# An adaLN transformer block in float32: the normalization's inverse root by GpSimd's power, and five product banks of the gated unit as one ring

## The chip, the core and the metric

The kernel runs on one core of a Trainium2 chip. A core has a matrix engine (TensorE, PE in the profile; its weight loads are listed apart as PEld), a vector engine (VectorE, DVE), a scalar engine for table functions (ScalarE, ACT), a general engine (GpSimd, POOL) and a queue engine (SyncE, SP). Each engine takes its instructions in order from its own queue, and they wait for one another by semaphores. [...] The metric is the time of one execution on the device in microseconds, as the median of several runs.

## What is computed

A block of a transformer with 2048 tokens of width 576: a conditioned layer normalization, full attention with 32 heads of width 18, a residual, a second conditioned normalization, a gated linear unit with 4608 hidden columns, and a second residual. All arrays are float32. Cut to what matters:

```python
def _layernorm(x, axis=-1, eps=1e-5):
    m = jnp.mean(x, axis=axis, keepdims=True)
    v = jnp.var(x, axis=axis, keepdims=True)
    return (x - m) / jnp.sqrt(v + eps)

mod = (_silu(c) @ w_mod).reshape(c.shape[0], 6, 1, -1)
sa, ca, ga, sb, cb, gb = (mod[:, i] for i in range(6))
h = _layernorm(x) * (1 + ca) + sa
qkv = h @ wqkv                                  # 32 heads of 18
p = softmax(q @ k.T * 18 ** -0.5)
x = x + ga * ((p @ v) @ wo)
h = _layernorm(x) * (1 + cb) + sb
x = x + gb * ((sigmoid(h @ w_gate) * (h @ w_up)) @ w_down)
```

## The kernel before

**Number format.** PE multiplies in a reduced float32 format, so most operands are split into a high part and a low part (the rest), and a product is made of three partial products.

**Start (the first 230 us).** Tokens lie in 16 tiles of 128 rows, four tiles to a chunk. `normalized(ch)` (L344) loads a chunk, takes mean and variance of each row on VectorE (`ln_stats`), the inverse root for the four tiles at once (`ln_scales`, L159, which runs `ln_scales_steps`, L163, to its end), and scales the rows (`ln_apply`, L179: VectorE at L181, and a small copy on GpSimd at L184). `ln_transpose` (L186) turns the chunk on PE (L192), and ScalarE and VectorE make from it the columns of `hT`. Then follow the projections to queries and keys (L274) and values (L325). PE's order in this stage is planned by the scheduler when the kernel is compiled: a list scheduler that takes instructions by priority, in the order of the program, as they come ready by its own estimates.

**Attention (about 230 to 1600 us).** 32 units of 16 steps. PE's order is written out by hand here (`manual_schedule` on PE, L888), by strings of letters in the loop at L906: `t` a score product (L927) with its exponential on ScalarE (L931), `m` a score product for the row maxima of a later unit (L446) with its reduction on VectorE (L452), `v` a group of eight value products (L548), and `w`, once in two steps, a turn of background work. All score products take their banks from a turn of seven. The background work is a set of generators; `first_rows` (L755) projects the attention's outputs of the first eight tiles, takes their statistics, calls `ln_scales_steps` for eight tiles at once (L762) and then normalizes and transposes the rows. Each `yield` in it hands the turn back.

**Gated unit (about 1600 us to the end).** The hidden columns are done in 18 blocks of 256, for each half of the tokens. A block's four quarter products are formed by seven products instead of eight, by sums and differences of operands, in the order `ORDER = (1, 6, 2, 7, 5, 4, 3)`; each is a gate product and an up product of seven matmuls (L1028), into two banks. `banks` (L1188) takes the pairs: `a` at product 1, accumulated again at 2 and read by the gate (L1037, L1038); `b_` at product 6, accumulated at 7 and 4 and read after each (L1212, L1223, L1234); `c` at product 5, accumulated at 3 and read after each (L1228, L1239). `a` and `c` come from a tag `x` with three banks, `b_` from two tags, `bg` and `bu`, with one bank each. The other three banks, tag `d`, take the down products (L1064), which VectorE adds to the result (L1068). Weights for a product are prepared three products ahead by GpSimd, ScalarE and VectorE (L1008, L1019, L1020, L1021) and in the first half stored for the second. PE's order is the scheduler's for the first 56 products (`ORDERED = 56`) and the program's from there on. In between, every second product, runs a generator `last_rows` (L1108): the output projection of the last columns, two calls of `ln_scales` (L1168) with four tiles each, and the operands of the second half.

**What the change touches.** `ln_scales_steps`, which is called seven times (four chunks at the start, once in attention, twice in `last_rows`); the two constants at L69; the loop at L762 that steps it in attention; and `banks` with its three callers. In `ln_scales_steps` the variance plus 1e-5 goes to `var` (VectorE), ScalarE takes its square root, and VectorE the reciprocal `r0` and one Newton step for the inverse root, `rs = r0 (1.5 - 0.5 var r0^2)`.

Of the kernel before, what the change touches and what calls it, by code (L numbers as in the profile page):

```python
# [15 lines left out]
F32 = mybir.dt.float32  # L16
F32R = mybir.dt.float32r
AF = mybir.ActivationFunctionType
ALU = mybir.AluOpType
# [4 lines left out]
P = 128  # L24
# [10 lines left out]
EPS = 1e-5  # L35
# [20 lines left out]
def tile_block(ctx, tc, x_in, wqkv, wo, w_gate, w_up, w_down, c_in, w_mod, out):  # L56
    nc = tc.nc
# [3 lines left out]
    const = ctx.enter_context(tc.tile_pool(name="const", bufs=1))  # L61
# [4 lines left out]

    ident = const.tile([P, P], F32, name="ident")
    make_identity(nc, ident)
    eps = const.tile([P, 1], F32, name="eps")  # L69
    nc.vector.memset(eps, EPS)  # L70
    mcol = const.tile([P, 2, 5], F32, name="mcol")
    mcol2 = const.tile([P, 2, 6], F32, name="mcol2")
    gb_b = const.tile([P, D], F32, name="gb_b")
# [9 lines left out]
    def bank():  # L83

        turns["bank"] += 1
        return ps.tile([P, 512], F32, name=f"s{turns['bank'] % 7}")
# [66 lines left out]
    def ln_stats(pool, xt, mv):  # L153
        st = pool.tile([P, 2, nc.vector.BN_STATS_DIM], F32, name="st", bufs=2)
        for g in range(2):
            nc.vector.bn_stats(st[:, g, :], xt[:, g, :] if len(xt.shape) == 3 else xt[:, g * HALF : (g + 1) * HALF])
        nc.vector.bn_aggr(mv, st)
# [5 lines left out]
    def ln_scales_steps(pool, mv, rs):  # L163

        n = rs.shape[-1]
        var = pool.tile([P, n], F32, name="var")
        nc.vector.tensor_scalar_add(var, mv[:, :, 1], EPS)
        sd = pool.tile([P, n], F32, name="sd")
        nc.scalar.activation(sd, var, AF.Sqrt)
        yield  # L170
        r0 = pool.tile([P, n], F32, name="r0")
        nc.vector.reciprocal(r0, sd)

        nc.vector.tensor_mul(sd, r0, r0)
        nc.vector.tensor_mul(sd, sd, var)
        nc.vector.tensor_scalar(sd, sd, -0.5, 1.5, op0=ALU.mult, op1=ALU.add)
        nc.vector.tensor_mul(rs, r0, sd)

    def ln_apply(z, xt, mean, rs):  # L179

# [206 lines left out]
    def temp(shape, dtype):  # L387
        temps["n"] += 1
        return qpool.tile(shape, dtype, name=f"t{temps['n'] % 2}")
# [113 lines left out]
    with tc.tile_pool(name="wv1", bufs=1) as wvp:  # L503
        tiles = [[(o + D * w, P)] for o in (128, 256, 384) for w in (0, 1)] + [[(DM, 64), (D + DM, 64)]]
        for i, parts in enumerate(tiles):
# [5 lines left out]
            for g in range(2):  # L511
                pl = project_qk([(wt, 2 * g), (wt, 2 * g + 1)], run if i else None)
                col, n = parts[-1]
# [20 lines left out]
    bgp = bgs.enter_context(tc.tile_pool(name="bgp", bufs=1))  # L534
# [65 lines left out]
    mv2 = const.tile([P, NT, 2], F32, name="mv2")  # L600
    rs2 = const.tile([P, NT], F32, name="rs2")
# [153 lines left out]
    def first_rows():  # L755
        yield from load_wo()
        for t in range(8):
            yield from project_o(t)
        for t in range(8):
            ln_stats(bgp, Oa[:, t, :], mv2[:, t, :])  # L760
            yield
        for _ in ln_scales_steps(bgp, mv2[:, 0:8, :], rs2[:, 0:8]):  # L762
            yield
            yield
        yield

        def normalized_part(i, g, r):

            z = bgp.tile([P, 4, P], F32, name="z", bufs=2)
            c0 = g * HALF + i * P  # L770
            for j in range(4):
                t = 4 * r + j
                if i < 2:
                    to, x1 = z[:, j, :], Oa[:, t, c0 : c0 + P]
                else:
                    to = z[:, j, :].rearrange("p (n c) -> p n c", c=32)
                    x1 = Oa[:, t, c0 : c0 + 32].unsqueeze(1).to_broadcast([P, 4, 32])
                nc.gpsimd.tensor_scalar(
                    to, x1, mv2[:, t, 0:1], rs2[:, t : t + 1], op0=ALU.subtract, op1=ALU.mult
                )  # L780
            return z

        held = {"n": 0}

        def parts():
            n = held["n"] = held["n"] + 1
            return held["parts"][n % 3] if n % 3 < 2 else bgp.tile([P, 2, 512], F32R, name="ho")

        order = [(i, g, r) for i in range(3) for g in range(2) for r in range(2)]
        z = normalized_part(*order[0])  # L790
        yield
        for n, (i, g, r) in enumerate(order):
            if not g and not r:
                four = temp([P, 4, 512], F32)
                ho = temp([P, 4, 512], F32R)
            pt = bank()
            for j in range(4):
                nc.tensor.transpose(pt[:, j * P : (j + 1) * P], z[:, j, :], ident)
            c = 3 * g + i
            nc.vector.tensor_scalar(  # L800
                four[:, 2 * g + r, :], pt, mcol2[:, 0, c : c + 1], mcol2[:, 1, c : c + 1],
                op0=ALU.mult, op1=ALU.add,
            )
            if n + 1 < len(order):
                z = normalized_part(*order[n + 1])
            yield
            if g and r:
                held["parts"] = ho[:, 0:2, :], ho[:, 2:4, :]
                blocks = [four[:, j, :] for j in range(4)] + [bgp.tile([P, 512], F32, name="t3")]
                yield from operand_parts(  # L810
                    0, i, blocks, parts, nc.gpsimd.tensor_copy, nc.gpsimd, nc.gpsimd
                )
# [79 lines left out]
    for u in range(UNITS):  # L892
# [6 lines left out]
        for kt in range(NT):  # L899
# [6 lines left out]
            for does in (("vtmmttmvtm", "tmttkwmtmm") if plain else ("vmmttmmtvt", "mtkttmwmmt"))[kt % 2]:  # L906
# [16 lines left out]
                else:  # L923
                    c, h = next(sides)
# [8 lines left out]
            if u in (1, 3):  # L933
                if kt == 2:
                    a = big.tile([P, 8, 640], F32, name="big")
                    a = a.rearrange("p a b -> p (a b)")[:, 0 : 8 * D].rearrange("p (t c) -> p t c", t=4)
# [109 lines left out]
    def down_weights(st):  # L1046
        wd = wdp.tile([P, 2, 2, D], F32R, name="wd")
        nc.sync.dma_start(wd.rearrange("p l t d -> p (l t d)").bitcast(F32), wds[st["b"]].bitcast(F32))
        st["wd"] = wd[:, 0], wd[:, 1]
# [44 lines left out]
    def prepare(n):  # L1094
        if n < len(seq):
            weights_operand(block(n), seq[n][2])
            at = n % 7
            if at in (1, 3):
                load(n // 7 + 1, at // 2)
# [5 lines left out]
    pg = ctx.enter_context(tc.tile_pool(name="pg", bufs=1, space=PSUM))  # L1105
# [79 lines left out]
                    nc.sync.dma_start(t, hs[g, i, :, cols])  # L1185
                yield from operand_parts(1, i, blocks, parts, nc.scalar.copy, nc.vector, nc.sync)

    def banks(*names):  # L1188
        return [pg.tile([P, 512], F32, name=n, bufs=3 if n == "x" else 1) for n in names]

    def half(t, v):
        return t[:, 512 * v : 512 * (v + 1)]
# [3 lines left out]
    for n, (hf, b, k) in enumerate(seq):  # L1196
        if n == ORDERED:
            manual.enter_context(tc.manual_schedule(engines={mybir.EngineType.PE}))
        prepare(n + LOOK)
        st = block(n)  # L1200
        if k == 1:
            st["a"] = banks("x", "x")
            product(st, 1, st["a"], True)
            st["p1"] = ep.tile([P, 1024], F32, name="p1")
            for v in range(2):
                nc.scalar.copy(half(st["p1"], v), st["a"][v])
        elif k == 6:
            st["b_"] = banks("bg", "bu")
            product(st, 6, st["b_"], True)
            st["u2"] = ep.tile([P, 1024], F32, name="u2")  # L1210
            for v in range(2):
                nc.vector.tensor_add(half(st["u2"], v), st["b_"][v], half(st["p1"], v))  # L1212
        elif k == 2:
            product(st, 2, st["a"], False)
            for r in range(2):
                st["hh", r] = ep.tile([P, 2, 512], F32R, name=f"hh{r}")
                st["hl", r] = ep.tile([P, 2, 512], F32R, name=f"hl{r}")
            gate(st, None, 0, 0)
        elif k == 7:
            product(st, 7, st["b_"], False)  # L1220
            st["u3"] = ep.tile([P, 1024], F32, name="u3")
            for v in range(2):
                nc.vector.tensor_add(half(st["u3"], v), st["b_"][v], half(st["p1"], v))  # L1223
        elif k == 5:
            st["c"] = banks("x", "x")
            product(st, 5, st["c"], True)
            for v in range(2):
                nc.vector.tensor_add(half(st["u3"], v), st["c"][v], half(st["u3"], v))  # L1228
            gate(st, st["u3"], 1, 1)
            down_weights(st)  # L1230
        elif k == 4:
            product(st, 4, st["b_"], False)
            for v in range(2):
                nc.vector.tensor_add(half(st["p1"], v), st["b_"][v], half(st["p1"], v))  # L1234
            gate(st, st["p1"], 1, 0)
        else:
            product(st, 3, st["c"], False)
            for v in range(2):
                nc.vector.tensor_add(half(st["u2"], v), st["c"][v], half(st["u2"], v))  # L1239
            gate(st, st["u2"], 0, 1)  # L1240
        if n >= 5 and n % 2:
            next(rows2, None)
        if before is not None and k in (6, 7):
            down(before, k - 6)
        if k == 3:
            before = st
        if hf == 0 and b == NB - 1:
            s = ORDER.index(k)
            nc.gpsimd.dma_start(X[s], xs[1, s])
# [30 lines left out]
```

## Time and profile before

| what | value |
|---|---|
| median of 3 runs | 2932.16 us (2930.02 to 2932.91) |
| the profiled execution's own time | 2929.86 us |
| its span, first to last instruction | 2927.5 us |
| instructions | 46356 |
| mean granted clock of TensorE | 0.995 |
| bytes moved by DMA | 429.25 MB |

By stage, from the profile's stretches (us busy of each stretch):

| stretch, us | PE | VectorE | ScalarE | GpSimd |
|---|---|---|---|---|
| 0 to 30 | 15.4 | 17.8 | 9.3 | 10.7 |
| 30 to 100 | 67.1 | 45.2 | 25.5 | 19.6 |
| 100 to 270 | 164.7 | 107.3 | 53.5 | 39.5 |
| 270 to 1000 | 719.0 | 651.6 | 650.0 | 213.9 |
| 1000 to 1605 | 596.3 | 499.6 | 505.2 | 173.5 |
| 1605 to 1700 | 86.7 | 72.0 | 28.7 | 24.2 |
| 1700 to 1850 | 147.8 | 123.4 | 56.6 | 39.2 |
| 1850 to 2200 | 332.4 | 282.9 | 118.8 | 100.8 |
| 2200 to 2927.5 | 718.9 | 418.9 | 133.8 | 28.0 |

How to read the profile's lines. A group has the line of the program, the engine, the operation, out <- in with partitions x elements, the count, then busy time in us and the mean of one in ns, and last the idle time of the engine just before these instructions and what ended it. A row of the timeline begins with its start and its duration in us; the bracket at its end is the time that the engine stood idle before it and what released it. A row of waits has the total in us, how often, and the longest. A row of the stretches has the stretch and its length, then the busy time of PE, PEld, VectorE, ScalarE and GpSimd with the count of instructions, the granted clock of TensorE (1.00 is full speed), the busy share of the DMA engines and GB/s. The ends of matmuls are modelled, and a busy PE isn't PE at its peak.

### The profile page before, as it was taken

The numbers are of one execution on the slowest core, as the hardware profiler recorded it, in microseconds if no ns is written. First come the engines' busy times: TensorE is split into PE (matmuls) and PEld (weight loads), VectorE is DVE, ScalarE is ACT, GpSimd is POOL, SyncE is SP. The second block draws the span as 40 slices with busy tenths as digits, with TensorE's granted clock in tenths as the row PEclk, the third lists the DMA queues.
The fourth block names the chain that finished last, engine by engine and source line by source line (L and its number), as shares of the span: only waits on it lengthen the run. The fifth ranks groups of instructions, "written<-read, shape, count | busy, mean of one in ns | idle before, by whom it ended". The sixth has DMA issues, their size and how long they took to land.

```text
span 2927.5 us, 46356 instructions
## 1 busy us (share of the span) xinstructions
PE 2848.3 (97%) x17141; PEld 1879.6 (64%) x17141; DVE 2218.6 (76%) x4023; ACT 1581.4 (54%) x2955; POOL 649.4 (22%) x829
## 2 busy tenths in 40 slices
PE   7999999999999999999999899999999999999998
PEld 6964333333444444444443788877888888888888
DVE  7277888888899988999982878789777555555555
ACT  3216889999987778998788333333332111111111
POOL 3122014544213110761102222233221100000000
PEclk9999999999999999999999999999999999999999
DMA  5344124333212110222125866677556844554443
GB/s 180 120 157 128 52 76 140 133 120 123 84 56 76 35 56 23 101 98 66 52 87 177 284 216 234 231 277 247 207 201 233 301 170 167 167 168 167 159 159 136
DMA packets 136745, 429.25 MB, mean 147 GB/s; under 512 B 18884, under 2 KB 56520, under 8 KB 124232
## 3 DMA queue, kind: packets, MB, share of 16 engines
q1 hardware_dynamic: 120472, 344.99, 35.0%
q0 software_dynamic: 16048, 81.31, 7.9%
q8 instruction: 135, 2.21, 0.3%
q14 instruction: 90, 0.74, 0.1%
HBM read 267.77 MB, written 157.95 MB: 145 GB/s over the span
## 4 chain that ended last, share of the span: by engine, by line
PE 82%; DVE 7%; ACT 4%; DMA 3%; issue 3%; SPq 1%; POOL 0%; POOLq 0%; ACTq 0%; DVEq 0%
PE o L548 16%; PE d L1064 14%; PE x L1028 12%; PE s L446 11%; PE s L927 10%; PE bu L1028 4%; PE bg L1028 4%; PE s L274 4%; ACT p L931 3%; PE s L325 2%; PE s L685 2%; DVE mx L452 1%; DVE w L1020 1%; DMA B<-hs 1%; PE s L572 1%
## 5 line engine op out<-in xcount | busy, mean ns | idle before, releaser
L452 DVE TENSOR_REDUCE mx<-s 128x1 f32<-128x512 f32 x1696 | 1076.6, 684 | 126.3 <-PE s L446 108.3
L931 ACT ACTIVATE p<-s 128x512 f32<-128x512 f32 x2048 | 1068.4, 610 | 146.7 <-PE s L446 75.2
L446 PE MATMUL s<-k,q 54*128 54x512 f32 x1920 | 608.4, 451 | 12.2 <-ACT p L931 6.6
L548 PE MATMUL o<-p,vaug 128*32 128x512 f32 x4096 | 554.8, 607 | 0.5 <-ACT p L931 0.4
L927 PE MATMUL s<-q,k 56*128 56x512 f32 x1920 | 552.6, 425 | 1.3 <-DMA q<-mrows 0.8
L1064 PE MATMUL d<-wd,hh 128*128 128x288 f32 x2304 | 468.3, 297 | 20.8 <-DVE Oa L1068 20.2
L927 PEld LDWEIGHTS s<-q,k 56*128 56x128 f32 x1920 | 260.5, 186 | 295.2 <-DVE mx L452 184.7
L446 PEld LDWEIGHTS s<-k,q 54*128 54x128 f32 x1920 | 273.6, 184 | 250.3 <-ACT p L931 172.3
L1064 PEld LDWEIGHTS d<-wd,hh 128*128 128x128 f32 x2304 | 373.4, 188 | 35.6 <-DVE Oa L1068 26.4
L1068 DVE TENSOR_TENSOR Oa<-Oa,d 128x288 f32<-128x288 f32 x576 | 256.0, 452 | 125.5 <-PE d L1064 120.3
L1064 PE MATMUL d<-wd,hl 128*128 128x288 f32 x1152 | 340.7, 296 | 0.0
L1028 PE MATMUL x<-k,w 128*128 128x512 f32 x1008 | 242.4, 390 | 4.7 <-DVE u L1239 2.4
L1040 ACT ACTIVATE u<-u 128x512 f32<-128x512 f32 x72 | 45.5, 632 | 318.3 <-DVE u L1228 312.1
L1064 PEld LDWEIGHTS d<-wd,hl 128*128 128x128 f32 x1152 | 216.9, 188 | 0.0
L1028 PEld LDWEIGHTS x<-k,w 128*128 128x128 f32 x1008 | 186.7, 188 | 42.5 <-DVE u L1239 3.5
L548 PEld LDWEIGHTS o<-p,vaug 128*32 128x32 f32 x4096 | 83.4, 108 | 163.9 <-issue 151.4
L1037 ACT ACTIVATE sg<-x 128x512 f32<-128x512 f32 x36 | 21.5, 599 | 304.3 <-PE x L1028 304.3
L1070 POOL DMA_DIRECT2D out_dram<-Oa x16 | 8.7, 543 | 606.0 <-DVE Oa L1068 606.0
L455 ACT ACTIVATE over<-s 128x512 f32<-128x512 f32 x176 | 105.1, 597 | 33.5 <-PE s L446 28.4
L1028 PE MATMUL x<-big,w 128*128 128x512 f32 x504 | 120.6, 390 | 1.0 <-issue 1.0
L1028 PE MATMUL x<-w,w 128*128 128x512 f32 x504 | 121.0, 390 | 0.0
L457 DVE CUSTOM_DVE_ANT_0 over<-s,over 128x512 f32<-128x512 f32 x176 | 120.2, 683 | 0.3
(232 smaller groups left out, 3605.1 us busy)
## 6 DMA issues: line engine op xcount, KB each, us to landing
ws<-w SPq DMA_DIRECT2D x126, 640.0 KB
w<-ws SPq DMA_DIRECT2D x126, 640.0 KB
wd<-wds SPq DMA_DIRECT2D x36, 1152.0 KB
k<-kd SPq DMA_DIRECT2D x60, 360.0 KB
wds<-w POOLq DMA_DIRECT2D x18, 1152.0 KB, 4.5
k<-kd SPq DMA_DIRECT2D x60, 180.0 KB
w<-in_B_w_down_dram POOLq DMA_DIRECT2D x18, 576.0 KB, 4.3
q<-qd SPq DMA_DIRECT2D x64, 144.0 KB
```

The source lines that it names most:

```text
L274: nc.tensor.matmul(acc, w, hT[:, t, cols], start=n == 0, stop=n == len(ts_) - 1)
L325: nc.tensor.matmul(acc[:, 0:HALF], hT[:, k, rows], w, start=n == 0, stop=n == len(ts_) - 1,)
L446: nc.tensor.matmul(sp, qs[rows, qt * P : (qt + 1) * P], ks[rows, at * 512 : (at + 1) * 512], start=True, stop=True,)
L452: nc.vector.tensor_reduce(to, sp, axis=AX.X, op=ALU.max)
L455: nc.scalar.activation(over, sp, AF.Relu)
L457: nc.vector.tensor_tensor_reduce(out=over, in0=sp, in1=over, scale=1.0, scalar=LOWEST, op0=ALU.add, op1=ALU.max, accum_out=mx[:, h * n + q ...
L548: nc.tensor.matmul(acc[32 * j : 32 * j + 32, :], vaug[:, kt, (2 * p + h) * VW : (2 * p + h) * VW + 32], probs[2 * c + h], start=kt == 0, s ...
L927: nc.tensor.matmul(sT, ks[rows, kcols], qs[rows, c * 512 : (c + 1) * 512], start=True, stop=True)
L931: state["exp"] = nc.scalar.activation(pr, sT, AF.Exp, scale=SCALE)
L1028: nc.tensor.matmul(acc[v], w[:, v, a, :], X[s][:, b, :], start=first and n == 0, stop=n == 6, skip_group_check=not first,)
L1064: nc.tensor.matmul(acc[:, :HALF], a[:, f, rows], w[:, f, cols], start=n == 0, stop=n == 5)
L1068: nc.vector.tensor_add(Oa[:, t, cols], Oa[:, t, cols], acc[:, :HALF])
```

## The change

The Sqrt activation and the reciprocal are replaced by one GpSimd instruction that raises `var` to the power in a constant tile `powers` (-0.5, eight columns, filled once by GpSimd at the start; the unused `eps` tile goes). Its result `r0` is refined by two Newton steps on VectorE instead of one, eight instructions in place of four and the reciprocal. The generator now yields after the power and after each Newton step; in attention the loop that yielded twice for each of its steps becomes a plain `yield from`, so that the turns from the variance to the first normalized part are three, as before. The five banks of the products get one tag: pairs are taken from five banks in the order of the program.

```diff
-    eps = const.tile([P, 1], F32, name="eps")
-    nc.vector.memset(eps, EPS)
+    powers = const.tile([P, 8], F32, name="powers")
+    nc.gpsimd.memset(powers, -0.5)
...
         var = pool.tile([P, n], F32, name="var")
+        sd = pool.tile([P, n], F32, name="sd")
+        r0 = pool.tile([P, n], F32, name="r0")
         nc.vector.tensor_scalar_add(var, mv[:, :, 1], EPS)
-        sd = pool.tile([P, n], F32, name="sd")
-        nc.scalar.activation(sd, var, AF.Sqrt)
+        nc.gpsimd.tensor_tensor(r0, var, powers[:, 0:n], op=ALU.pow)
         yield
-        r0 = pool.tile([P, n], F32, name="r0")
-        nc.vector.reciprocal(r0, sd)
-
-        nc.vector.tensor_mul(sd, r0, r0)
-        nc.vector.tensor_mul(sd, sd, var)
-        nc.vector.tensor_scalar(sd, sd, -0.5, 1.5, op0=ALU.mult, op1=ALU.add)
-        nc.vector.tensor_mul(rs, r0, sd)
+        for to in (r0, rs):
+            nc.vector.tensor_mul(sd, r0, r0)
+            nc.vector.tensor_mul(sd, sd, var)
+            nc.vector.tensor_scalar(sd, sd, -0.5, 1.5, op0=ALU.mult, op1=ALU.add)
+            nc.vector.tensor_mul(to, r0, sd)
+            yield
...
-        for _ in ln_scales_steps(bgp, mv2[:, 0:8, :], rs2[:, 0:8]):
-            yield
-            yield
-        yield
+        yield from ln_scales_steps(bgp, mv2[:, 0:8, :], rs2[:, 0:8])
...
-    def banks(*names):
-        return [pg.tile([P, 512], F32, name=n, bufs=3 if n == "x" else 1) for n in names]
+    def banks():
+        return [pg.tile([P, 512], F32, name="x", bufs=5) for _ in range(2)]
...
-            st["a"] = banks("x", "x")
+            st["a"] = banks()
...
-            st["b_"] = banks("bg", "bu")
+            st["b_"] = banks()
...
-            st["c"] = banks("x", "x")
+            st["c"] = banks()
```

## The prediction

> **What bounds the kernel now.** I began with the busy times on the profile's page.
>
> ```profile
> PE 2848.3 (97%) x17141; PEld 1879.6 (64%) x17141; DVE 2218.6 (76%) x4023; ACT 1581.4 (54%) x2955; POOL 649.4 (22%) x829
> ```
>
> TensorE (PE) is busy for 97% of the span, and every other engine has room. Work taken from ScalarE (ACT) or added to VectorE (DVE) or GpSimd (POOL) therefore counts only where PE waits for it; only some 80 us of the span are PE idle. So I went to the places of the two edits. First the groups of ScalarE, where the square root shows by its table loads.
>
> ```profile
> L169 ACT ACT_TABLE_LOAD x4 | 5.1, 1283 | 0.1
> L931 ACT ACT_TABLE_LOAD x2 | 2.6, 1283 | 4.0 <-DMA kd<-kd_p 4.0
> L1037 ACT ACT_TABLE_LOAD x2 | 2.6, 1283 | 0.0
> ...
> L1040 ACT ACT_TABLE_LOAD x1 | 1.3, 1283 | 0.0
> ```
>
> L169 is the Sqrt. Its four loads go, and with them the loads that bring back Exp (one of L931's two) and Sigmoid (one of L1037's two and that of L1040): seven loads of 1.283 us, 9.0 us of ScalarE. Whether PE feels them is read from the timeline. Only one pair lies in the attention stage:
>
> ```profile
> 1107.95 1.28 ACT L169 ACT_TABLE_LOAD   x1
> 1109.24 0.21 ACT L169 ACTIVATE sd<-var 128x8 f32<-128x8 f32 x1
> 1109.47 1.28 ACT L931 ACT_TABLE_LOAD   x1
> 1110.76 0.60 ACT L931 ACTIVATE p<-s 128x512 f32<-128x512 f32 x1
> ```
>
> For 2.8 us no exponential runs. The timeline of PE over the same time shows what that does; x8 is one group of value products, two of which belong to each pair of steps.
>
> ```profile
> 1103.79 1.06 PE L548 MATMUL o<-p,vaug 128*32 128x512 f32 x8
> ...
> 1108.84 1.06 PE L548 MATMUL o<-p,vaug 128*32 128x512 f32 x8
> 1109.83 0.49 PE L927 MATMUL s<-q,k 56*128 56x512 f32 x1
> 1111.41 0.50 PE L446 MATMUL s<-k,q 54*128 54x512 f32 x1 [1.09 <-ACT p L931]
> ...
> 1117.37 1.07 PE L548 MATMUL o<-p,vaug 128*32 128x512 f32 x8
> ```
>
> A pair of steps takes 1108.84 - 1103.79 = 5.05 us; the pair with the table loads takes 1117.37 - 1108.84 = 8.53 us. So 3.5 us are lost there, though PE's one marked wait is 1.09 us. The rest shows in the stretches by window (the seventh number is the granted clock):
>
> ```profile
> 33.00:37.00 4.00, 3.91 (x16) 3.92 (x17) 4.00 (x19) 0.30 (x2) 0.01 (x1) 0.50 0.76 270
> 1113.00:1117.00 4.00, 4.00 (x17) 1.45 (x19) 2.36 (x6) 2.28 (x5) 4.00 (x6) 0.57 0.02 4
> 1605.00:1700.00 95.00, 86.68 (x474) 74.86 (x473) 71.97 (x123) 28.69 (x41) 24.23 (x23) 1.00 0.80 273
> ```
>
> After the stall the clock was 0.57 for four microseconds: a stall is followed by slow matmuls.
>
> **The change, part by part.** *Sqrt out, in the attention stage.* Both loads and the Sqrt leave ScalarE: -3.5 us by the two cadences (by ScalarE's own 2.8 us alone it would be -2.8). The other Sqrt loads lie at the start (ScalarE then waits for inputs) and in the gated stage, where ScalarE is idle most of the time, so I give them nothing; without that cover each would cost PE its 1.28 us.
>
> [...]
>
> *The power in.* The trace has no power on GpSimd. The nearest rows are an ordinary two-input instruction and GpSimd's longest single one:
>
> ```profile
> L591 POOL TENSOR_TENSOR Oa<-oT,rec 128x144 f32<-128x144 f32 x32 | 13.1, 433 | 171.2 <-ACT oT L587 170.9
> ...
> L364 POOL MEMSET vaug<- 128x9936 f32 x1 | 8.4, 8383 | 0.0
> ```
>
> A power of 4 or 8 elements per partition takes p, between under 0.43 and 8.4 us. In size it is nearest to the first row, but a power is many operations per element, so I take p = 1.0 us for every site and keep both ends. It is issued on POOL's in-order queue, which is mostly empty at each of the seven sites (22% busy). The new wait is on VectorE: the first Newton product waits for POOL where the reciprocal waited for ScalarE. Behind it on VectorE's queue stand, by stage, the normalization itself, the row maxima (which free PE's score banks) and the adds of the down products (which free PE's bank ring d). In attention the wait before was
>
> ```profile
> 1109.48 0.20 DVE L172 RECIPROCAL r<-sd 128x8 f32<-128x8 f32 x1 [0.29 <-ACT sd L169]
> ```
>
> so 0.7 us may be added at p = 1; the row maxima have some play, and I take +0.4 (0 to 0.7).
>
> *Newton's second step.* Eight VectorE instructions follow where there were five:
>
> ```profile
> L177 DVE TENSOR_TENSOR rs<-r,sd x7: 145/161/168, 10.7 to 1842.3; 128x4 f32<-128x4 f32 x6, 128x8 f32<-128x8 f32 x1
> ```
>
> Three more at 0.16 us are 0.5 us per site. The chain from variance to scale grows by p - 0.2 (the Sqrt) + 0.5 = 1.3 us. At the start this chain feeds PE's transposes of each chunk through the last POOL copy:
>
> ```profile
> 11.54 1.71 POOL L184 COPY x<-x 128x64 f32<-128x64 f32 x4 [1.96 <-DVE x L181]
> ...
> 36.99 1.71 POOL L184 COPY x<-x 128x64 f32<-128x64 f32 x4 [23.74 <-DVE x L181]
> 50.24 1.71 POOL L184 COPY x<-x 128x64 f32<-128x64 f32 x4 [11.54 <-DVE x L181]
> ...
> 65.48 1.70 POOL L184 COPY x<-x 128x64 f32<-128x64 f32 x4 [4.95 <-DVE x L181]
> ```
>
> ```profile
> 18.62 0.77 PE L192 MATMUL s<-ident,x 128*128 128x128 f32 x5
> ...
> 39.08 2.35 PE L192 MATMUL s<-ident,x 128*128 128x128 f32 x20
> ...
> 51.89 2.34 PE L192 MATMUL s<-ident,x 128*128 128x128 f32 x20
> ...
> 67.86 2.34 PE L192 MATMUL s<-ident,x 128*128 128x128 f32 x20
> ```
>
> The copies end at 13.25, 38.70, 51.95 and 67.18, so the transposes have 5.4, 0.4, 0 and 0.7 us to spare: 1.3 us more makes them late by 0, 0.9, 1.3 and 0.6, together 2.8. PE's order here is planned when the kernel is compiled, and value projections that need no new chunk can go ahead of the transposes, so I take half, +1.4 (0 to 2.8).
>
> [...]
>
> At the last rows, in the gated stage, two sites get 0.5 us more of VectorE each. VectorE already makes PE wait there:
>
> ```profile
> PE d L1064 <- DVE Oa L1068: 20.2, 22, 2.9
> ```
>
> I take +0.5 (0 to 2.6, if the 0.8 us of waiting for the power is paid too). In attention the three instructions are hidden: VectorE is 76% busy.
>
> *The ring.* Pairs of banks are taken in the order a, b_, c. Before, bank a[1] of a block reused the bank of c[0] of the block before, which is read only after product 3, the product just ahead; with five in turn b_[1] follows c[0], one product later, and no other bank gets a shorter lead than it had. The timeline has this wait once, at the first change of block:
>
> ```profile
> 1620.02 1.89 PE L1028 MATMUL bu<-big,w 128*128 128x512 f32 x7 [2.65 <-DVE u L1223]
> ...
> 1629.62 0.69 DVE L1239 TENSOR_TENSOR u<-x,u 128x512 f32<-128x512 f32 x1
> ...
> 1630.37 1.89 PE L1028 MATMUL x<-k,w 128*128 128x512 f32 x7 [2.38 <-DVE u L1239]
> ...
> 1635.51 0.63 PE L1124 MATMUL d<-ident,od 128*128 128x128 f32 x4 [1.66 <-DMA od<-oend]
> ```
>
> PE would save 2.4 us at 1630.37. But what is late next is the transpose at 1635.51, which waits for a load, seen in the chain of waits:
>
> ```profile
> 1628.49 6.89 DMA od<-oend
> ```
>
> It is issued by SP's queue at 1628.49 and lands at 1635.4 whatever the ring does; PE would wait there 4.0 us instead of 1.7. So I take 0. The other wait (2.65 us) is for reading a bank before its next accumulation, which a ring doesn't change. Yet PE's order of the first 56 products is planned at compile time, and another bank rule gives another order. The ends: both waits vanish (-5.0), or as much is added (+5.0); the stretch from 1605 to 1700 holds 95 - 86.7 = 8.3 us of PE idle in all.
>
> *Sum:* -3.5 + 0.4 + 1.4 + 0.5 + 0 = -1.2 us. The profiled execution took 2929.86 us (span 2927.5), which is 2.3 us under the median of 2932.16 and just under the lowest run shown, 2930.02. Against its own time the forecast is 2928.7; against the median, 2931.0, and that is my number.
>
> **Rivals.** *A, the ring pays (faster).* The new order of the first products removes both waits: -1.2 - 5.0, and the chunks at the start are filled wholly (-1.4): 2924.6 us. For it: the bank waits stand in the trace. Against: the load that is late next.
>
> *B, the power is slow (slower).* Every site has VectorE waiting in order behind POOL. By the terms above the time grows with p: attention p - 0.3, half of the three unspared chunks (3 (p + 0.3) - 1.1) / 2, half of two last sites p + 0.3, less 3.5: together 3.5 p - 3.6. It cancels the gain at p = 1.0, is slower by over 0.2% from p = 2.7, and at p = 4 gives +10.4, 2942.6 us; at 8.4 it gives 2958. For it: POOL has no such operation in the trace, and 1 us is only chosen. Against: few elements.
>
> *C, the start stalls and the clock falls.* PE's wait before 33.09 was followed by a clock of 0.50 from 33 to 37, 2 us of lost work:
>
> ```profile
> 33.09 0.85 PE L325 MATMUL s<-wv_h,hT 128*128 128x288 f32 x2 [2.62 <-DVE pl L281]
> ```
>
> If nothing fills the chunks (2.8 instead of 1.4) and two of the three late transposes are followed by such a stretch, that is 5.4 us more: 2936.4; with a worse order of the first products, up to 2941.4.
>
> *D, the loads stay*, because another function needs the table that the Sqrt brought in: +3.5, 2934.5. Against: between the sites only Exp, or only Sigmoid, is table-bound.
>
> **How the numbers follow.** A measurement of this kernel can tell about 0.2%, 5.9 us, from no change; that is 2926.3 to 2938.0. The forecast has 0.38, A 0.24, B 0.22, C 0.14, D 0.02. Faster is A, 0.24. Slower is B and most of C (0.10), 0.32. Within 0.2% are the forecast, the rest of C and D, 0.44. The forecast's own range, with its unknown costs at p near 1, is 2926 to 2936. The range for 8 in 10 reaches to A on one side and to B with p up to 5 (+13.9) on the other: 2922 to 2948.
>
> **What would show it.** Three table loads instead of ten; the pair of steps around 1109 us at about 5 us and no clock under 0.9 there; a POOL power group with a mean near 1 us, seven times; transposes L192 within 2 us of where they were; at block 1 no wait of `x` for the add into u2, and a longer wait of the `od` transposes. Wrong would be: a power of several us with VectorE idle behind it (B), a clock near 0.5 between 37 and 80 us (C), a quite different order of products before the fifty-sixth (A or its opposite).

## The result, and the profile after

The changed kernel took 2937.20 us (median of 12 runs, 2932.38 to 2941.66), the kernel before 2931.49 (12 runs beside them, 2929.28 to 2935.0). The ratio is 1.0021 with a 95% interval of 1.0012 to 1.0030: the change costs about 6 us where 1.2 us of gain were forecast.

| what | before | after |
|---|---|---|
| profiled execution | 2929.86 us | 2937.07 us |
| its span | 2927.5 us | 2935.3 us |
| table loads on ScalarE | 10 | 3 |
| mean granted clock of TensorE | 0.995 | 0.992 |

The lines are numbered three lower in the new kernel from the attention on (L1025 is the old L1028, L928 the old L931). First the page's busy times, and the groups of ScalarE and GpSimd.

```profile
PE 2854.3 (97%) x17141; PEld 1887.8 (64%) x17141; DVE 2220.5 (76%) x4043; ACT 1570.8 (54%) x2941; POOL 660.4 (22%) x837
```

```profile
L341 ACT ACT_TABLE_LOAD x1 | 1.3, 1283 | 4.9 <-DMA craw<-in_c_dram 4.9
L928 ACT ACT_TABLE_LOAD x1 | 1.3, 1283 | 4.0 <-DMA kd<-kd_p 4.0
L1034 ACT ACT_TABLE_LOAD x1 | 1.3, 1283 | 0.0
```

```profile
L170 POOL TENSOR_TENSOR r<-var,powers 128x4 f32<-128x4 f32 x6 | 6.9, 1142 | 27.2 <-DVE var L169 19.4 <-PE x L1025 7.8
L170 POOL TENSOR_TENSOR r<-var,powers 128x8 f32<-128x8 f32 x1 | 1.7, 1681 | 10.7 <-DVE var L169 10.7
```

The seven loads are gone, and the power takes 1.14 us on average for four columns and 1.68 for eight, near the 1.0 chosen. Both forecasts of what the instructions are were right, so the next question is what waits for them. VectorE's waits for the power, all together:

```profile
DVE sd L173 <- POOL r L170: 7.8, 7, 1.8
```

Seven waits, 7.8 us, all on an engine that takes its instructions in order. Now the sites one by one. At the start, VectorE's timeline of the first chunk:

```profile
10.70 0.16 DVE L173 TENSOR_TENSOR sd<-r 128x4 f32<-128x4 f32 x1 [1.38 <-POOL r L170]
...
11.29 0.16 DVE L176 TENSOR_TENSOR r<-r,sd 128x4 f32<-128x4 f32 x1
18.91 0.42 DVE L134 COPY mrow<-s 128x256 f32<-128x256 f32 x1 [7.46 <-PE s L121]
19.25 0.15 DVE L173 TENSOR_TENSOR sd<-r 128x4 f32<-128x4 f32 x1
...
20.49 2.04 DVE L181 TENSOR_SCALAR x<-x,mv,rs 128x576 f32<-128x576 f32 x4
```

The first Newton step ends at 11.45. The second is ready, but the planner put it behind L134, a copy that waits for PE's modulation products; VectorE idles for 7.46 us with the second step queued behind. The rows are scaled at 20.49 instead of 10.90. The second chunk on VectorE:

```profile
39.33 0.15 DVE L176 TENSOR_TENSOR r<-r,sd 128x4 f32<-128x4 f32 x1
39.39 0.46 DVE L156 BATCH_NORM_STATS2 st<-x 128x6 f32<-128x288 f32 x1
39.76 0.15 DVE L173 TENSOR_TENSOR sd<-r 128x4 f32<-128x4 f32 x1
...
40.27 0.15 DVE L174 TENSOR_TENSOR sd<-sd,var 128x4 f32<-128x4 f32 x1
40.33 0.46 DVE L156 BATCH_NORM_STATS2 st<-x 128x6 f32<-128x288 f32 x1
40.70 0.16 DVE L175 TENSOR_SCALAR sd<-sd 128x4 f32<-128x4 f32 x1
```

Each instruction of 0.15 us alternates with statistics of the next chunk of 0.46 us, so a step costs some 1.9 us here (39.33 to 41.20), not four times 0.16. PE shows the consequence:

```profile
21.12 4.19 PE L192 MATMUL s<-ident,x 128*128 128x128 f32 x20 [0.75 <-DVE x L181]
...
42.12 4.04 PE L192 MATMUL s<-ident,x 128*128 128x128 f32 x20 [2.03 <-DVE x L181]
56.31 2.34 PE L192 MATMUL s<-ident,x 128*128 128x128 f32 x20
72.29 2.35 PE L192 MATMUL s<-ident,x 128*128 128x128 f32 x20
```

They began at 18.62, 39.08, 51.89 and 67.86 before. The first two groups after the change also run slow: the second takes 4.04 us where it took 2.35 before. In the stretches by window the clock is the number before the last two:

```profile
21.00:26.00 5.00, 4.74 (x22) 3.94 (x22) 4.08 (x12) 1.93 (x3) 3.17 (x4) 0.66 0.86 249
33.00:37.00 4.00, 2.07 (x10) 1.55 (x11) 3.99 (x14) 1.07 (x2) 0.10 (x1) 1.00 0.02 4
...
42.00:47.00 5.00, 4.88 (x26) 4.71 (x27) 3.45 (x13) 1.71 (x3) 2.67 (x5) 0.66 0.23 61
```

The landing of the first modulation weights varies by more than 2 us between executions, so I measure the start from the copy L134, which it releases by way of PE's products, to the first reduction to `nm`. Before:

```profile
18.74 0.42 DVE L134 COPY mrow<-s 128x256 f32<-128x256 f32 x1 [5.79 <-PE s L121]
201.66 0.21 DVE L464 TENSOR_REDUCE nm<-mx 128x16 f32<-128x64 f32 x1
```

That is 182.92 us; after it is 206.09 - 18.91 = 187.18: the start is 4.3 us longer. In attention, VectorE and then PE after the change:

```profile
1107.39 0.17 DVE L169 TENSOR_SCALAR var<-mv 128x8 f32<-128x8 f32 x1
1109.35 0.17 DVE L173 TENSOR_TENSOR sd<-r 128x8 f32<-128x8 f32 x1 [1.79 <-POOL r L170]
1109.44 1.88 DVE L452 TENSOR_REDUCE mx<-s 128x1 f32<-128x512 f32 x3
```

```profile
1105.81 1.06 PE L548 MATMUL o<-p,vaug 128*32 128x512 f32 x8
...
1110.17 0.49 PE L446 MATMUL s<-k,q 54*128 54x512 f32 x2 [1.62 <-DVE mx L452]
1110.60 1.92 PE L548 MATMUL o<-p,vaug 128*32 128x512 f32 x8
...
1114.03 1.07 PE L548 MATMUL o<-p,vaug 128*32 128x512 f32 x8
```

VectorE stands for 1.79 us before the first Newton product; the row maxima queue behind it; PE waits 1.62 us for the bank that they free (the tile of 128x512 that a product goes to), and the next group of products takes 1.92 us instead of 1.06. From 1105.81 to 1114.03 are 8.22 us, two groups that without a stall lie 3.16 + 1.89 = 5.05 apart: 3.2 us are lost where the table loads lost 3.5. One stall was exchanged for another. In the gated stage, PE at the first change of block:

```profile
1637.15 1.09 PE L1121 MATMUL d<-ident,od 128*128 128x128 f32 x4 [4.85 <-DMA od<-oend]
1637.89 1.20 PE L1025 MATMUL x<-k,w 128*128 128x512 f32 x2
...
1639.60 2.48 PE L1025 MATMUL x<-k,w 128*128 128x512 f32 x5
```

The wait of `x` for the add into u is gone, and the wait for the `od` load grew from 1.66 to 4.85, as the forecast had it (4.0). What it lacked: after this wait the matmuls run slow, in a stretch with a granted clock of 0.82:

```profile
1630.00:1640.00 10.00, 5.15 (x22) 4.15 (x21) 9.17 (x14) 4.25 (x7) 2.33 (x2) 0.82 1.00 319
```

Before, with two waits of 2.4 and 1.7 us in place of one, that stretch had 1.00:

```profile
1630.00:1640.00 10.00, 7.98 (x43) 6.59 (x44) 9.65 (x14) 4.25 (x7) 2.35 (x2) 1.00 1.04 325
```

The length of a wait alone doesn't tell what follows it here: the stretch with the wait of 4.85 us had a clock of 0.82, that with the waits of 2.4 and 1.7 us 1.00, and in attention a wait of 1.62 us was followed by a group of 1.92 us, at a clock of 0.58 from 1110 to 1114 us. Nor is a slow stretch certain there: in the trace of `pow_chunk0_first`, one of the runs below, the same wait of 1.62 us was followed by a group of 1.06 us, and two groups that lie 8.22 us apart here lay 6.68 apart, 1.6 us more than without a stall.

### The profile page after: what moved, and what is told of

The parts are those of the page before. It is cut to its first block, busy times and chain, and to the rows that moved or that the text cites. A ratio compares the mean times of both kernels' runs of the same rounds, so it can differ in the third digit from the quotient of the medians.

```text
span 2935.3 us, 46406 instructions
## 1 busy us (share of the span) xinstructions
PE 2854.3 (97%) x17141; PEld 1887.8 (64%) x17141; DVE 2220.5 (76%) x4043; ACT 1570.8 (54%) x2941; POOL 660.4 (22%) x837
## 3 DMA queue, kind: packets, MB, share of 16 engines
q8 instruction: 135, 2.21, 0.3%
## 4 chain that ended last, share of the span: by engine, by line
PE 81%; DVE 7%; ACT 4%; issue 4%; DMA 2%; SPq 1%; POOL 0%; POOLq 0%; DVEq 0%; ACTq 0%
PE x L1025 20%; PE o L548 16%; PE d L1061 14%; PE s L446 11%; PE s L924 10%; PE s L274 4%; ACT p L928 3%; PE s L325 2%; PE s L685 2%; DVE mx L452 1%; DVE w L1017 1%; PE s L572 1%; DVE hl L1041 1%; DMA B<-hs 1%; DVE w L1018 1%
## 5 line engine op out<-in xcount | busy, mean ns | idle before, releaser
L928 ACT ACTIVATE p<-s 128x512 f32<-128x512 f32 x2048 | 1068.8, 610 | 147.1 <-PE s L446 79.4
L1025 PE MATMUL x<-k,w 128*128 128x512 f32 x1512 | 361.1, 393 | 2.4 <-ACT w L1016 2.4
L1025 PEld LDWEIGHTS x<-k,w 128*128 128x128 f32 x1512 | 284.2, 190 | 59.5 <-ACT w L1016 2.6
L1025 PE MATMUL x<-big,w 128*128 128x512 f32 x1008 | 236.1, 390 | 2.0 <-issue 1.0
L1025 PE MATMUL x<-w,w 128*128 128x512 f32 x1008 | 236.1, 390 | 0.0
L1025 PEld LDWEIGHTS x<-big,w 128*128 128x128 f32 x1008 | 188.6, 188 | 41.8 <-issue 1.4
L1025 PEld LDWEIGHTS x<-w,w 128*128 128x128 f32 x1008 | 187.0, 188 | 36.7
```

The source lines that it names most:

```text
L928: state["exp"] = nc.scalar.activation(pr, sT, AF.Exp, scale=SCALE)
L1025: nc.tensor.matmul(acc[v], w[:, v, a, :], X[s][:, b, :], start=first and n == 0, stop=n == 6, skip_group_check=not first,)
```

## The experiments

The theory: the power's cost is VectorE's in-order queue, at the start and in attention, and the ring alone costs little (V in the expectations). Rivals: the ring makes the loss (R); it is only where the slow clock happens to fall (L). Differences below are ratio minus one, times 2930 us, against runs of the kernel before on the same chip; their intervals are about 2.6 us to each side (3.2 and 3.7 for the two runs of `pow_ends`, which have 9 and 5 executions). The sixteen measurements were taken in four sets on three chips.

**Each half alone.** `pow_alone` takes back the banks, `ring_alone` takes back the normalization. The edit of `pow_alone` against the changed kernel, without the three callers (`ring_alone` has the reverse edit against the kernel before):

```diff
-    def banks():
-        return [pg.tile([P, 512], F32, name="x", bufs=5) for _ in range(2)]
+    def banks(*names):
+        return [pg.tile([P, 512], F32, name=n, bufs=3 if n == "x" else 1) for n in names]
...
```

> The whole of the normalization's change with the banks of before. Theory V (VectorE's in-order queue pays for the power, the ring is neutral): about +4.1 us against before, made of +4.4 at the start (first chunk's transposes at about 21.1 us, second chunk's at about 42.1), -0.3 in attention, 0 in the gated unit. Rival R (the ring and its order of the first products make the loss): 0 to -1. Rival L (the difference is only where slow clock happens to fall): anything within +-3 with the start no later than before. Under V the od load is waited for 1.7 us at the first block change, as before.

> Sqrt as before, the five product banks as one ring. Theory V: 0 to +2 us; the start as before, no wait of x for the add into u at the first block change, the od wait 4.0 to 4.9 us instead of 1.7. Rival R: +4 to +6, all of it after 1600 us. Rival L: within +-3 with no site of its own.

`pow_alone`: 1.0018 (1.0009 to 1.0027), +5.3 us. `ring_alone`: 1.0006 (0.9997 to 1.0015), +1.8 us. The normalization makes most of the loss, and R falls. V doesn't come out whole either: it put all of the loss before 80 us, and the start of `pow_alone` is 2.8 us longer than before; where the rest lies is seen by sites below. Whether the ring costs anything the total of `ring_alone` doesn't tell, as zero lies within its interval; its trace does. In it the `od` wait is 4.20 us and the clock behind it 0.66:

```profile
1632.78 1.08 PE L1124 MATMUL d<-ident,od 128*128 128x128 f32 x4 [4.20 <-DMA od<-oend]
```

```profile
1630.00:1640.00 10.00, 7.22 (x30) 6.36 (x31) 9.27 (x15) 2.67 (x4) 3.41 (x3) 0.66 0.86 293
```

From the first copy of a product (`p` from `x` on ScalarE) in the first block to that in the third, the time is 72.1 us before, 74.1 after, 73.2 in `ring_alone`; of the thirteen profiles below and above with the old banks and the power somewhere, none took over 72.5.

**The power by sites.** `pow_attention` has it in attention alone, `pow_ends` at the start and the last rows, `pow_start` and `pow_last` at one of these each; elsewhere the code of before. The edit is which of two bodies `ln_scales` has:

```diff
     def ln_scales(pool, mv, rs):
-        for _ in ln_scales_steps(pool, mv, rs):
-            pass
...
+        nc.vector.tensor_scalar_add(var, mv[:, :, 1], EPS)
...
+        nc.scalar.activation(sd, var, AF.Sqrt)
...
+        nc.vector.reciprocal(r0, sd)
...
```

> Power and two Newton steps only where attention uses them; Sqrt and one step at the start and at the last rows, banks of before. Theory V: -0.3 to 0 us, since one stall (scale late through table loads) goes and another (row maxima queued behind a VectorE wait of about 1.8 us for GpSimd) comes; PE waits about 1.6 us for a row maximum. The prediction's term of -3.1 is the rival: PE with no wait over 0.5 us there, -3.1 us.

> Power and two Newton steps at the four chunks of the start and at the two sites of the last rows; Sqrt in attention, banks of before. Theory V: +4.4 us, all of it before 80 us; transposes of the first chunk at about 21.1, of the second at about 42.1, both 2 to 3 us late. The prediction's start term is the rival: +1.4 at the start and +0.5 at the last rows, +1.9 us.

> Power and two steps only at the four chunks of the start. Measured from the copy that ends the first modulation (it waits for a load whose landing varies by 2 us between executions) to the first row maxima's reduction near 201 us, kernels with Sqrt took 182.9 to 183.5 us and those with the power 185.7 to 187.2. Theory V: 185.7 to 187.2 here too, +2.8 to +4.1, and about that in total. The prediction's +1.4 is the rival.

> Power and two steps only at the two sites of the last rows. Theory V: +0.5 to +1.5 us in total; between 1752 and 1790 us PE waits about 0.2 twice for z and some 0.7 for a down product's add. Rival (the ends' loss of 7.3 us lies half in the last rows): +3 or more.

| kernel | ratio (95%) | us | again | us | copy to `nm`, us |
|---|---|---|---|---|---|
| `pow_attention` | 0.9992 (0.9983 to 1.0001) | -2.3 | | | 183.5 |
| `pow_ends` | 1.0025 (1.0014 to 1.0036) | +7.3 | 1.0034 (1.0022 to 1.0047) | +10.0 | 186.5, 187.1 |
| `pow_start` | 1.0002 (0.9993 to 1.0010) | +0.6 | 1.0010 (1.0002 to 1.0019) | +2.9 | 187.1, 186.7 |
| `pow_last` | 1.0001 (0.9992 to 1.0010) | +0.3 | 1.0009 (1.0000 to 1.0017) | +2.6 | 183.4, 183.0 |

The columns "again" are repeats on one chip, asked because the first `pow_ends` and the first two parts alone didn't add up:

> The power at the start and at the last rows once more, beside each of the two alone on one chip. Theory V: start 185.7 to 187.2 us from the copy, total +4 to +6 against before. Rival (the first measurement of +7.3 and the start's +0.6 differ because the loss at the start is given back later or depends on when the first loads land): +1 to +2, the sum of the two alone as measured.

> The power at the start alone once more. Theory V: start 185.7 to 187.2 us from the copy, total +2.8 to +4.1 against before. Rival: +0.6 in total again though the start is as late.

> The power at the last rows alone once more. Theory V: +0.5 to +1.5 us. Rival: 0.3 or less, as in the first measurement.

In the traces the start agrees everywhere: all nine profiles with Sqrt there took 182.9 to 183.5 us, the six with the power and the planner's own order 185.7 to 187.2, on average 3.6 longer. At the first of the two sites of the last rows PE loses about 1.4 us: with the power alone there (`pow_last`, the repeat), then before,

```profile
1745.00:1795.00 50.00, 48.64 (x266) 41.87 (x265) 42.83 (x89) 18.89 (x28) 15.88 (x17) 1.00 0.65 226
```

```profile
1745.00:1795.00 50.00, 50.00 (x268) 42.69 (x267) 43.84 (x87) 22.48 (x33) 14.91 (x16) 1.00 0.67 237
```

and PE's waits in this trace of the repeat, from 1745 to 1795 us, name parts of it, a scaled row that comes late and an add into `Oa` behind it on VectorE:

```profile
PE d L1074 <- DVE Oa L1078: 0.7, 1, 0.7
PE d L720 <- DVE z L705: 0.4, 2, 0.2
```

The second site costs as well. I take the stretch from the first copy of a product in the fifth block to that in the ninth (1752.48 to 1903.24 us before), which holds both sites. There the nine profiles with the power at the last rows took 152.1 to 153.2 us, the nine with Sqrt 149.8 to 151.2. The difference of the averages is 2.1 us, 1.0 in the first two blocks and 1.1 in the next two, around the second site. Which wait makes the second part isn't shown: PE's marked waits from 1795 to 1866 us are 1.8 us before and 0.8 to 1.4 in the changed kernel and both runs of `pow_last`.

The totals follow less well: the parts alone average +1.8 and +1.5, together 3.2, the two at once 8.6. The repeats of `pow_ends` and `pow_last` came out above what V gave them; at first V had given the last rows nothing. The sites' 3.6 + 2.1 = 5.7 lie between. What is left stays open, and slow clock may be part of it: from 1903.24 to the block that begins at 2134.86 before, profiles with the power at the last rows took 232.6 to 236.9 us (clock 0.96 to 0.98) and those with Sqrt 231.5 to 234.7 (0.97 to 0.99). So L falls for the start and the two sites, where the ranges don't meet, and isn't excluded for the rest.

**The start, its two causes apart.** In `pow_chunk0_first` only the copies of the modulation row are queued behind the first chunk's scaled rows. In `pow_chain_first` they are queued behind the first chunk's second step, and each later chunk's statistics behind the scale of the chunk before. In `pow_one_step` the second Newton step goes, at all sites. Cut to what matters, the edits of the first and the last:

```diff
+            with tc.issue_after(held["x"]):
-            nc.vector.tensor_copy(row[:, 0:256], pm[:, 0:256])
+                nc.vector.tensor_copy(row[:, 0:256], pm[:, 0:256])
...
-        for to in (r0, rs):
+        for to in (rs,):
```

> The whole of the normalization's change, banks of before; only the copies of the modulation row are queued on VectorE behind the first chunk's scaled rows, everything else is left to the planner. Theory V: first transposes within 0.2 us of the copy as with Sqrt (2.2 us late without this); the second chunk's chain still alternates with statistics, so those transposes are 1.5 to 2.5 us later than with Sqrt and the start takes 184.3 to 185.5 us from the copy; total +3 to +4 against before. Rival (the first chunk alone makes the loss): start 183 to 183.5, total about +1.

> The whole of the normalization's change, banks of before; on VectorE the copies of the modulation row are queued behind the first chunk's second Newton step, and each chunk's statistics behind the scale of the chunk before. Theory V (the start is late because the second step stands behind a waiting copy in chunk 0, and because each of its instructions alternates with a 0.46 us statistics instruction in chunk 1): first transposes at about 18.7 us, the second chunk's at about 39.3, start +0.3 to +0.7 instead of +2.6 to +4.4, total +1 to +2 against before. Rival (a power and three more instructions cost this much in any order): start +2.6 to +4.4, total about +5.3.

> The power at all seven sites with one Newton step instead of two (four VectorE instructions where before had five), banks of before. Theory V: first transposes on time (18.7 us), the second chunk's 0.5 to 1.2 us late by the wait for the power, attention as before within 0.5, last rows +0.3: total +0.5 to +1.5 against before. Rival (the wait for GpSimd is the cost, not the second step): about +4 to +5.3, as with two steps.

`pow_chunk0_first`: 1.0004 (0.9996 to 1.0013), +1.2 us. Its first chunk's chain, with the copy behind it:

```profile
11.29 0.16 DVE L179 TENSOR_TENSOR r<-r,sd 128x4 f32<-128x4 f32 x1
11.49 0.17 DVE L176 TENSOR_TENSOR sd<-r 128x4 f32<-128x4 f32 x1
...
12.29 2.05 DVE L184 TENSOR_SCALAR x<-x,mv,rs 128x576 f32<-128x576 f32 x4
20.66 0.42 DVE L137 COPY mrow<-s 128x256 f32<-128x256 f32 x1 [6.32 <-PE s L123]
```

The copy waits as ever, but nothing stands behind it. The start took 204.63 - 20.66 = 183.97 us: of 3.6 us, 2.7 came from the first chunk. That lies between what I expected (184.3 to 185.5) and the rival (183 to 183.5). The second chunk's transposes speak for the rival: they came 20.5 us after the copy, as with Sqrt, so what is left for the alternation with statistics is 0.9 us at most. `pow_chain_first`: 1.0025 (1.0015 to 1.0034), +7.3: a miss. Its first chunk was half mended and its second wholly (0.97 and 20.18 us after the copy; 2.21 and 23.21 in the changed kernel, -0.12 and 20.34 before), but the third and fourth came 1.5 and 3.9 us late, because their statistics now stood behind the chain, and the whole start took 187.4. `pow_one_step`: 1.0007 (0.9998 to 1.0016), +2.1, start 184.0: without the second step most of the start's loss goes, though the power and its waits stay.

**Attention: the wait, not the power.** In `pow_attention`, with the Newton steps where the changed kernel has them, the stall is the same: VectorE waits 1.79 us and PE 1.62. `pow_attention_held` queues the Newton steps behind a row maximum some 20 us later; the edit is shown against the steps of the changed kernel.

```diff
-                    nc.vector.tensor_reduce(to, sp, axis=AX.X, op=ALU.max)
+                    state.setdefault("max", []).append(nc.vector.tensor_reduce(to, sp, axis=AX.X, op=ALU.max).ins)
...
+        yield
+        after = state["max"][-40]
         for to in (r0, rs):
-            nc.vector.tensor_mul(sd, r0, r0)
+            with tc.issue_after(after):
+                nc.vector.tensor_mul(sd, r0, r0)
```

> As the power in attention alone, but the eight Newton instructions are queued on VectorE some 37 instructions (about 20 us) later, behind a row maximum whose product comes that much later; the normalized rows are transposed only at 1170 us. Theory V (the stall is VectorE waiting in order for GpSimd, not the power itself): no VectorE wait for r, no PE wait over 0.5 us near 1107, no slow clock there, and the prediction's whole term: -3 us against before in this place, total -2.5 to -4. Rival (the two sites are worth nothing whatever the order): 0 to -1, as with the power in attention alone by its landmarks.

> The power in attention alone with the Newton steps queued later, once more. Theory V: -2.5 to -4 us against before. Rival (the first measurement of -4.4 was luck): 0 to -1.

0.9985 (0.9976 to 0.9994), -4.4 us, 2927.23 us median; again 0.9993 (0.9984 to 1.0002), -2.1 us. VectorE and PE at the site:

```profile
1106.32 0.17 DVE L178 TENSOR_SCALAR var<-mv 128x8 f32<-128x8 f32 x1
1106.40 1.88 DVE L464 TENSOR_REDUCE mx<-s 128x1 f32<-128x512 f32 x3
...
1126.55 0.15 DVE L185 TENSOR_TENSOR sd<-r 128x8 f32<-128x8 f32 x1
```

```profile
1104.74 1.06 PE L560 MATMUL o<-p,vaug 128*32 128x512 f32 x8
1107.90 1.06 PE L560 MATMUL o<-p,vaug 128*32 128x512 f32 x8
1109.79 1.07 PE L560 MATMUL o<-p,vaug 128*32 128x512 f32 x8
```

The maxima follow the variance at once, and the pair takes 5.05 us. Between the reductions to `nm` at 1065.59 and 1158.05 before lie 92.46 us; in the changed kernel 92.14, here 89.35 and 89.40. One pair of traces says little, since the stretch behind the stall isn't slow each time: the ten profiles with Sqrt in attention took 91.3 to 94.2 us, 93.0 on average, and the six with the power in the changed kernel's order 90.7 to 93.6, on average 92.2. The held order lies below all of them. So the prediction's -3.1 was there to be had, in this order. This kernel, with the power in attention alone and the banks of before, has the lowest average ratio of all tried. It is faster than the kernel before by its two measurements together (the second alone has 1 within its interval); that it is faster than `pow_attention` (0.9992) only the trace shows, not the totals.

**The ring's next wait.** `ring_od_early` issues the first `od` load from GpSimd's queue at about 1607 us; `ring_od_scalar` moves besides the three copies of its transposes to ScalarE.

```diff
-                nc.sync.dma_start(od[:, :, 0:192], oend[:, t0 : t0 + 4, :])
+                q = nc.sync if t0 else nc.gpsimd
+                q.dma_start(od[:, :, 0:192], oend[:, t0 : t0 + 4, :])
...
-                nc.vector.tensor_copy(oh, pt)
+                nc.scalar.copy(oh, pt)
```

> Sqrt as before, five banks as a ring, and the first load of od issued by GpSimd's queue at about 1605 us instead of by SP's at 1626, where it stands behind 20 us of stores. Theory V (the ring's gain of 2.4 us moves into the wait for this load): no od wait, no bank wait at the change of block, -3 to -4 us against before and -5 against the ring alone. Rival (some third thing, such as the weights' operands, is late next): within 1.5 us of before, with a wait of PE for w or S in place of od.

> As the ring with the early od load, and the three copies of od's transposes (oh, om, omh) done by ScalarE instead of VectorE. VectorE was busy for 19.3 of the 20 us from 1620 to 1640 in each of the three kernels looked at. Theory W (there VectorE is what ends last, so neither the bank wait nor the load was worth anything by itself): about 1.3 us of VectorE goes, PE's waits for ol and om (0.9 and 1.1 us) shrink by 1 us or more in sum, the stretch from block 1's first copy to block 2's gets shorter by about 1 us, total 1 us less than with the early load alone. Rival (the order of products itself costs): no difference.

`ring_od_early`: 1.0009 (1.0000 to 1.0019), +2.6 us, a miss. No wait for `od` is left, but PE's waits in `ring_od_early` from 1600 to 1680 are

```profile
PE x L1028 <- DVE u L1224: 3.2, 1, 3.2
PE d L1064 <- DVE om L1137: 1.1, 1, 1.1
PE d L1064 <- DVE ol L1129: 0.9, 1, 0.9
```

and its stretch from 1620 to 1640 shows why (VectorE is the third busy time):

```profile
1620.00:1640.00 20.00, 16.88 (x69) 13.57 (x69) 19.30 (x29) 9.26 (x14) 7.28 (x6) 0.83 0.69 240
```

VectorE works for 19.3 of 20 us, as it did before (19.35). With the bank and the load out of the way, PE next waits for VectorE. `ring_od_scalar`: 0.9997 (0.9989 to 1.0006), -0.9 us; the waits for `ol` and `om` are gone, an add into `Oa` is waited for 1.7 us instead, and blocks 1 to 3 take 72.2 us in place of 73.7. The waits for `ol` and `om` went as theory W had it, but PE's waits from 1600 to 1680 us didn't shrink in sum (5.2 and 5.4 us), VectorE is as busy as ever (19.28 of the 20 us), and the total is within no change from before: W isn't shown.

## Why the prediction was wrong

- **Sqrt out, -3.5 us: right in size, and not to be had as the change is written.** Seven loads went and the stall with them. Only the held order shows the gain, -3.1 us against the trace before and -3.7 against the average of the profiles with Sqrt.
- **VectorE's wait for the power in attention, +0.4 (0 to 0.7): the first step that failed.** The duration was right (1.68 us for eight columns); "the row maxima have some play" was not. With 1.79 us of waiting, PE waited 1.62 and then ran slow (clock 0.58 from 1110 to 1114 us): 3.2 us lost (1.3 to 4.2 in the six traces, on average 2.8). The old wait of 0.29 us had hidden that there is almost no play, and the prediction priced the wait alone, though it had itself shown a clock of 0.57 behind a stall of 1.09 us.
- **The start, +1.4 (0 to 2.8): the second step that failed.** Measured +3.6 (2.8 to 4.3). The slack of the first chunk, 5.4 us, was counted as if the new instructions would follow the old at once. The planner put them behind a copy that waits for PE, and the slack went into that wait: 2.7 us. The second step's four instructions also cost more than four times 0.16 us where they alternate with others.
- **Last rows, +0.5 (0 to 2.6):** about 2.1 over both sites, so mis-sized by four times, though within its bounds. The wait for the power, which the value of 0.5 left out, was paid: VectorE stood 0.95 and 0.78 us for it in the changed kernel.
- **Ring, 0 (-5.0 to +5.0):** the mechanism was right, the wait moved to the load. In the trace it costs about 2 us more, the slow clock at one long wait (0.82 with a wait of 4.85 us, 0.66 with 4.20 in `ring_alone`); the total of +1.8 has zero within its interval. The other wait, which a ring was not to change, shrank from 2.65 to 0.97 us in the changed kernel.
- **Rivals.** B had the sign and the mechanism (VectorE in order behind POOL) but put it down to a slow power; at p near 1 it gave nothing. C had the start's stall, and in part its slow clock: in the profile of after the first two late groups of transposes ran at 0.66. In `pow_alone` they were nearly as late and ran at 1.00, and the start was 1.4 us shorter, so the stall costs by itself. The stretch that C took as its example, 33 to 37 us, was slow before (0.50) and is not after (1.00). A and D fell.

With the measured sizes, from the sites: -0.9 in attention (92.2 against 93.0 us), +3.6 at the start, +2.1 at the last rows and +2 from the ring make +6.8, against +6 measured (3.5 to 8.8). That they meet so well is in part luck, as two measurements of `pow_ends` differ by 2.7 us.

## What to carry to other kernels

Before work is moved to an idle engine, look at who waits for the result and what is queued behind that waiting instruction: here VectorE waited 1.79 us for GpSimd with row maxima queued behind, and PE, the bound engine, waited 1.62 us for one of those. Place the consumer later in its queue where the result isn't needed yet; here that alone turned a stall into a gain of 3 us at that place. Slack that is read from a trace holds for the order in that trace: instructions that are added to a planned chain can land behind something that waits, as the second Newton step did here behind a copy that waited 7.46 us.

## What the runs showed of the hardware

- In the changed kernel the six powers of 128x4 took 1.01 to 1.53 us, 1.14 on average, and the one of 128x8 1.68. The first of them all showed no extra delay: in the profile of after it began at 9.61 us, at once behind POOL's earlier work, took 1.05 us, and VectorE went on at 10.70.
- ScalarE's pair of table loads and the power cost PE nearly the same in attention, 3.5 and 3.2 us in the profiles before and after, though one held back ScalarE and the other VectorE: PE's marked waits are 1.09 and 1.62 us of these. Much of the rest is the slow stretch behind them (clock 0.57 from 1113 to 1117 us before, 0.58 from 1110 to 1114 us after), which doesn't come each time: against the held order the ten profiles with Sqrt there lost 1.9 to 4.9 us and the six with the power 1.3 to 4.2.
- The landing of the modulation weights at the start varied by 2.7 us between the eighteen profiled executions (the copy L134 began between 18.5 and 21.2 us), more than some effects sought; a time counted from the event that the load releases is free of that.
